# A second pair of accumulator banks for tile 5 of a two-MLP kernel, and six tiles ahead of the transpositions

## The chip, the cores and the metric

The kernel runs on one core of a Trainium2 chip. The metric is the time of one execution in device microseconds (us). The median of three runs stands for the kernel.

## The reference

Linear attention with decay feeds two MLPs in a row. Batch 4, 8 heads, 768 positions, head dimension 64, so 3072 tokens of width 512; the first MLP has 1024 hidden columns, the second 2048. All in float32.

```python
for t in range(S):
    state = gamma * state + einsum('bhd,bhe->bhde', k[:, :, t], v[:, :, t])
    y[:, :, t] = scale * einsum('bhd,bhde->bhe', q[:, :, t], state)
# x: (3072, 512)
h = x @ w_in                                   # first MLP, 512 -> 1024
sm = exp(h - max(h)) / (sum(exp(h - max(h))) + 1e-09)
solu = h * sm
x = ((solu - mean) / sqrt(var + 1e-06) * g_ln) @ w_out    # 1024 -> 512
h = x @ w_in2                                  # second MLP, 512 -> 2048
out = (h * cos(h)) @ w_out2                    # 2048 -> 512
```

## The kernel before

**Tiles.** The 3072 tokens are 24 tiles of 128 tokens (24 steps of the attention, each two batches by 64 positions), and six blocks of four tiles. Each float32 factor is split in a high and a low part, and each product is three matmuls (high by high, low by high, high by low).

**What one tile does.** `both(n)` does on TensorE the scores of step n+1 and the state of step n; VectorE then masks the scores (`masks`, two instructions, tile `in`) and ScalarE copies the state (`state_copy`, two instructions, tile `in`). `att_out(n)` makes the attention's output `y`, VectorE scales it to `x`, and ScalarE and VectorE split it into `xh` and `xl`. `first(n, c)` is the first layer of the first MLP for half c of its columns: four calls of `mm1`, each three matmuls of 128x512 (L543), so 24 matmuls for a tile, into two accumulator banks. `norm(n)` is then the row-wise normalisation: the maximum on VectorE (L561), the exponential on ScalarE, the product of both on VectorE (the last reader of the banks, an L332 row `u<-u,hA` or `u<-u,hB`, with a short row that reads its sum out), and further steps on the copy `u` in SBUF. Once four tiles of a block are normalised, `transp(g, j)` (L588) transposes column group j of the block, four transpositions of 128x128 each, into one of two banks `tr0` and `tr1`, which ScalarE and VectorE split into `lt` (L597, L599). `mm2(g, d)` (L612) is the second layer.

**Banks.** The banks of tile n are `hA` (two banks), or `hB` (two more) for tiles 1 and 3. `hB` lives in a pool of its own (`psb`, in the exit stack `boot`). `open_tr` closes this pool, and the two banks `tr0` and `tr1` are allocated in the place that it gives back. All these pools are opened with `reuse_waits="tile"`: the first writer of a new tile waits for all accesses to the old tile whose place it takes. The other banks are `y1` (one) and, for the attention, `sc`, `S` and `y` (three).

**The order.** The functions issue nothing; they enter operations into a plan with their engine, a cost, and the names that they read and write. `Plan.order` then writes out one order for all engines, by a list schedule over these costs and names. Each engine executes its part strictly in that order; the waits in the finished program come from the tiles that are really touched, not from the plan's names. TensorE's operations are taken from a window of the next ten in the order in which the code enters them, and the one with the smallest key goes first:

```python
for k, i in enumerate(pe[:self.WINDOW]):        # WINDOW = 10
    if need[i] == 0:
        t = max(free[e], ready_at[i])
        c.append((max(free[e], ready_at[i] + self.MARGIN) + k * self.STEP, t, i))  # 0.3, 0.05
```

So an operation that stands k places behind the first costs k times 0.05 us, and may overtake if it is ready earlier by more than that. VectorE and ScalarE take what can start first, and of that what has the longest path behind it; where nothing of the tiles is ready they take weight conversions (`convert`: rows `top`, `big`, `raw`, `o1h`, `o1l`, `w2a`).

**The order around the change.** Tiles 0 to 2 are entered by hand, then a loop enters tiles 3 to `EARLY` - 1, each as `first(n, 0)`, `first(n, 1)`, `attend()`; `attend` enters `both` and `att_out` of the tile two further on. Then the blocks follow. For block g, four more tiles (as far as there are any) are entered in eight halves (`part()`), between the transpositions and second layers of block g:

```python
transp(g, 0); transp(g, 1); part(); transp(g, 2); transp(g, 3); part()
mm2(g, 0, None, range(4)); transp(g, 4); transp(g, 5); part(); transp(g, 6); transp(g, 7); part()
mm2(g, 0, None, range(4, 8)); part(); part(); mm2(g, 1); part(); mm2(g, 2, ...); part(); mm2(g, 3)
```

With `EARLY` = 5, tile 5 is entered between the first transpositions, and the last block that has tiles to go with it (block 4) has three. `open_tr` is a step of the plan without cost, put in as soon as the operations that name `hB` have begun.

Of the kernel before, what the change touches and what calls it, by code (L numbers as in the profile page):

```python
# [34 lines left out]
K2 = FF2 // 128  # L35
NBLK = NT // 512
LAG = 3
EARLY = 5
UBUF = 7

INV2PI = 1.0 / (2.0 * math.pi)
# [197 lines left out]
def body(ctx: ExitStack, tc: tile.TileContext, qkv, consts,  # L239
# [40 lines left out]
    hA = ps1.tile([128, 2, 512], F32, name="hA")  # L280
# [3 lines left out]
    hB = psb.tile([128, 2, 512], F32, name="hB")  # L284
# [242 lines left out]
    p2 = {}  # L527

    def hbank(n, c):
        return (hB if n in (1, 3) else hA)[:, c], (("hB", c) if n in (1, 3) else ("hb", c))  # L530

    def h_of(n):
        return hB if n in (1, 3) else hA

    def mm1(n, c, k, ms=(0, 1, 2)):
        h, hk = hbank(n, c)
        xh, xl = xhs[n % 2], xls[n % 2]
        s = slice(c * 512, (c + 1) * 512)

        def mm():  # L540
            for m in ms:
                a, w = ((xh, w1h), (xl, w1h), (xh, w1l))[m]
                nc.tensor.matmul(out=h, lhsT=a[:, k], rhs=w[:, k, s], start=(k + m == 0), stop=(k == KD - 1 and m == 2))  # L543
        r = [("xh", n % 2)]
        if 0 in ms or 1 in ms:
            r += [("w1h", k, c)]
        if 1 in ms:
            r += [("xl", n % 2)]
        if 2 in ms:
            r += [("w1l", k, c)]  # L550
        P.add("PE", 0.2267 * len(ms), mm, r, [hk], lat=0.2267 * len(ms) + 0.25)

    def norm(n):
        b = [hbank(n, c) for c in (0, 1)]
        h = h_of(n)
        hk = [b[0][1], b[1][1]]
        sm = sms[n % 3]
        smk = lambda *c: [("sm", n % 3, x) for x in c]
        u = us[n % UBUF]
        uk = [("u", n % UBUF, c) for c in (0, 1)]  # L560
        P.add("DVE", 1.135, lambda: nc.vector.tensor_reduce(  # L561
            out=sm[:, 0:1], in_=h, axis=AX.XY, op=ALU.max, negate=True), hk, smk(0))
        act(u, h, AF.Exp, hk + smk(0), uk + smk(1), 1.1, 1.35, bias=sm[:, 0:1], accum_out=sm[:, 1:2])
        stt(u, u, 1.0, h, ALU.mult, ALU.mult, hk, uk + smk(2), 1.18, accum_out=sm[:, 2:3])
        ts(sm[:, 3:4], sm[:, 2:3], -1.0 / FF1, None, ALU.mult, None, smk(2), smk(3), 0.07)
        act(junk, u, AF.Square, uk + smk(3), [("junk",)] + smk(4), 1.14, 1.38, bias=sm[:, 3:4], accum_out=sm[:, 4:5])
        ts(sm[:, 5:6], sm[:, 1:2], 1e-9, None, ALU.add, None, smk(1), smk(5), 0.07)
        stt(sm[:, 6:7], sm[:, 5:6], 1e-6, sm[:, 5:6], ALU.mult, ALU.mult, smk(5), smk(6), 0.07, port=True)
        stt(sm[:, 7:8], sm[:, 4:5], 1.0 / FF1, sm[:, 6:7], ALU.mult, ALU.add, smk(4, 6), smk(7), 0.07, port=True)
        P.add("POOL", 0.56, lambda: nc.gpsimd.tensor_tensor(out=sm[:, 8:9], in0=sm[:, 7:8], in1=mhalf, op=ALU.pow),  # L570
              smk(7), smk(8), port=True)
        tt(sm[:, 9:10], sm[:, 3:4], sm[:, 8:9], ALU.mult, smk(3, 8), smk(9), port=True, occ=0.07)
        act(u, u, AF.Identity, smk(8, 9), uk, 1.14,
            alt=("DVE", 0.75, lambda: nc.vector.tensor_scalar(
                out=u, in0=u, scalar1=sm[:, 8:9], scalar2=sm[:, 9:10], op0=ALU.mult, op1=ALU.add), True),
            scale=sm[:, 8:9], bias=sm[:, 9:10])
# [214 lines left out]
    def attend():  # L791
        n = nxt[0]
        if n >= ns:
            return
        nxt[0] += 1
        if n == 0:
            load_to(0)
            prep(0)
            scores(0)
        load_to(n + 1)  # L800
        if n + 1 < ns:
            prep(n + 1)
            both(n)
        att_out(n)
        if n == ns - 1:
            p2["sb_hook"] = [P.add("HOOK", 0.0, open_sb, lat=0.0, after=P.using({"in", "amg", "sc", "S", "y"}))]

    def first(n, c):
        for k in range(KD):
            mm1(n, c, k)  # L810
        if c == 1:
            norm(n)
# [46 lines left out]
    attend()  # L859
    for n in range(3, EARLY):  # L860
        first(n, 0)
        first(n, 1)
        attend()
    nb = EARLY
    for g in range(NBLK - 1):
# [132 lines left out]
```

## Time and profile before

| | us |
|---|---|
| median of 3 runs | 900.62 |
| lowest and highest run | 896.74, 902.73 |
| the profiled execution, its own time | 899.53 |
| its span, first to last instruction | 897.7 |
| TensorE busy in it | 873.6 |

PE is TensorE's matmuls, DVE is VectorE, ACT is ScalarE, POOL is GpSimd, SP issues most DMAs. Times of rows are us from the start of the span unless marked ns. The profiled execution lies 1.1 us below the median.

### The profile page before, as it was taken

To read this page: it belongs to the slowest core of one execution; us is meant where nothing else is said; L and a number is where in the kernel's file an instruction comes from. 1 tells how busy PE (TensorE), PEld (TensorE's weight loads), DVE (VectorE), ACT (ScalarE), POOL (GpSimd) and SP (SyncE) were. 2 spreads that over 40 slices of the span, in tenths; PEclk is the share of its full clock that TensorE was granted. 3 is DMA by queue.
4 is the path that set the end of the run, shared out by engine and by line. 5 is a ranking of instruction groups with operands and counts; after the bars stand their busy time and mean duration, and the time that the engine had idled before them with its cause. 6 is when DMAs were issued, how large, how long until landed. Compare 5 with 4: busy or idle time off the path is not lost.

```text
span 897.7 us, 14593 instructions
## 1 busy us (share of the span) xinstructions
PE 873.6 (97%) x5888; PEld 722.6 (80%) x5888; DVE 571.2 (64%) x1014; ACT 421.5 (47%) x701; POOL 45.9 (5%) x62
## 2 busy tenths in 40 slices
PE   5998999999999999999999999999999999999997
PEld 4777888888888878888888888888888888888886
DVE  4989858587473665476656565656655565557553
ACT  4688746466452464353343343334433443334332
POOL 2111201011010000000000000000000000000000
PEclk9998999999999999999999999999999999999999
DMA  9993688888520141220020002001200120011002
GB/s 265 295 336 96 189 276 269 296 254 297 161 81 32 50 139 65 82 106 1 24 71 0 1 24 71 0 1 46 49 1 0 48 47 1 1 48 24 1 0 48
DMA packets 38660, 85.17 MB, mean 95 GB/s; under 512 B 5440, under 2 KB 5440, under 8 KB 38592
## 3 DMA queue, kind: packets, MB, share of 16 engines
q1 hardware_dynamic: 38224, 83.24, 29.9%
q10 hardware_dynamic: 368, 0.99, 0.4%
q8 instruction: 46, 0.75, 0.3%
q14 instruction: 22, 0.18, 0.1%
HBM read 64.29 MB, written 19.92 MB: 94 GB/s over the span
## 4 chain that ended last, share of the span: by engine, by line
PE 90%; DMA 4%; DVE 2%; ACT 2%; issue 0%; SPq 0%; ACTq 0%
PE h L681 29%; PE acc L718 29%; PE y L612 12%; PE hA L543 11%; DMA in<-qkv_dram 4%; PE tr L612 2%; PE tr L588 2%; PE y L455 2%; PE sc L390 1%; DMA big<-w_in_dram 1%; ACT junk L321 1%; ACT u L321 0%; DVE in L324 0%; DVE u L332 0%; DVE sm L561 0%; PE S L398 0%
## 5 line engine op out<-in xcount | busy, mean ns | idle before, releaser
L693 ACT ACTIVATE r<-r,hp 128x512 f32<-128x512 f32 x96 | 69.5, 724 | 158.8 <-DVE r L691 158.8
L695 DVE TENSOR_TENSOR r<-r,h 128x512 f32<-128x512 f32 x96 | 66.0, 687 | 65.2 <-ACT r L693 65.2
L612 PE MATMUL y<-lt,o1h 128*128 128x512 f32 x320 | 105.3, 397 | 0.7 <-ACT ys L617 0.7
L687 DVE SCALAR_TENSOR_TENSOR r<-ki,h 128x512 f32<-128x512 int32 x96 | 65.9, 686 | 56.4 <-ACT ki L685 56.4
L699 DVE TENSOR_TENSOR gl<-r,gh 128x512 fp32r<-128x512 f32 x96 | 66.3, 690 | 46.3 <-ACT gh L697 46.3
L718 PE MATMUL acc<-o2u,gh 128*128 128x512 f32 x288 | 94.5, 389 | 0.0
L718 PE MATMUL acc<-o2h,gh 128*128 128x512 f32 x240 | 93.4, 389 | 0.0
L718 PE MATMUL acc<-o2h,gl 128*128 128x512 f32 x240 | 93.4, 389 | 0.0
L718 PE MATMUL acc<-o2l,gh 128*128 128x512 f32 x240 | 93.4, 389 | 0.0
L685 ACT ACTIVATE ki<-h 128x512 int32<-128x512 f32 x96 | 57.4, 598 | 75.1 <-PE h L681 75.1
L697 ACT ACTIVATE gh<-r 128x512 fp32r<-128x512 f32 x96 | 60.5, 630 | 53.0 <-DVE r L695 53.0
L543 PE MATMUL hA<-w1h,xh 128*128 128x512 f32 x176 | 72.2, 410 | 8.9 <-DVE u L332 6.9
L681 PE MATMUL h<-yh,w1h 128*128 128x512 f32 x192 | 74.7, 389 | 0.0
L681 PE MATMUL h<-yh,w1l 128*128 128x512 f32 x192 | 74.7, 389 | 0.0
L681 PE MATMUL h<-yl,w1h 128*128 128x512 f32 x192 | 74.7, 389 | 0.0
L612 PEld LDWEIGHTS y<-lt,o1h 128*128 128x128 f32 x320 | 60.0, 188 | 14.6 <-ACT ys L617 1.2
L543 PE MATMUL hA<-w1h,xl 128*128 128x512 f32 x176 | 69.0, 392 | 0.0
L543 PE MATMUL hA<-w1l,xh 128*128 128x512 f32 x176 | 68.6, 394 | 0.0
L689 DVE SCALAR_TENSOR_TENSOR r<-ki,r 128x512 f32<-128x512 int32 x96 | 66.4, 691 | 3.1
L718 PEld LDWEIGHTS acc<-o2u,gh 128*128 128x128 f32 x288 | 54.0, 188 | 11.2
L612 PE MATMUL y<-lt,o1l 128*128 128x512 f32 x160 | 62.3, 390 | 0.0
L681 PE MATMUL h<-yh,w2a 128*128 128x512 f32 x192 | 59.5, 391 | 0.0
(108 smaller groups left out, 1687.6 us busy)
## 6 DMA issues: line engine op xcount, KB each, us to landing
in<-qkv_dram SPq DMA_DIRECT2D x48, 256.0 KB, 5.1
in<-qkv_dram SPq DMA_DIRECT2D x95, 128.0 KB, 4.7
raw<-w_in_dram SPq DMA_DIRECT2D x16, 511.8 KB, 6.1
raw<-w_out_dram SPq DMA_DIRECT2D x16, 511.8 KB, 4.7
y1d<-ys SPq DMA_DIRECT2D x24, 256.0 KB, 2.5
x<-y1d SPq DMA_DIRECT2D x24, 256.0 KB, 3.1
out_dram<-o SPq DMA_DIRECT2D x48, 128.0 KB, 2.4
kept_out<-wt SPq DMA_DIRECT2D x16, 256.0 KB, 3.6
```

The costliest lines, as they stand in the source:

```text
L455: nc.tensor.matmul(out=p_y[64 * par:64 * par + 64, j], lhsT=W[par][:, j], rhs=X[par][:, j], start=True, stop=True)
L543: nc.tensor.matmul(out=h, lhsT=a[:, k], rhs=w[:, k, s], start=(k + m == 0), stop=(k == KD - 1 and m == 2))
L612: nc.tensor.matmul(out=y1(), lhsT=w[:, j, ds], rhs=lts[j][:, a], start=(j + m == 0), stop=(j == K1 - 1 and m == 2))
L681: nc.tensor.matmul(out=p2["h2"][b], lhsT=w2tile(c, lo)[:, k, cs], rhs=p2[a][:, k], start=(k + m == 0), stop=(k == KD - 1 and m == 2))
L685: P.add("ACT", 0.5, lambda: nc.scalar.activation(out=p2["ki"][s], in_=p2["h2"][b], func=AF.Identity, scale=INV2PI, bias=0.25), [("h2", b)] ...
L687: P.add("DVE", 0.61, lambda: V.scalar_tensor_tensor(out=p2["r"][s], in0=p2["ki"][s], scalar=-C1, in1=p2["h2"][b], op0=ALU.mult, op1=ALU.ad ...
L689: P.add("DVE", 0.61, lambda: V.scalar_tensor_tensor(out=p2["r"][s], in0=p2["ki"][s], scalar=-C2, in1=p2["r"][s], op0=ALU.mult, op1=ALU.add ...
L693: P.add("ACT", 0.62, lambda: nc.scalar.activation(out=p2["r"][s], in_=p2["r"][s], func=AF.Sin, bias=hp[:, 0:1]), (), [("r", s)])
L695: P.add("DVE", 0.6, lambda: V.tensor_tensor(out=p2["r"][s], in0=p2["r"][s], in1=p2["h2"][b], op=ALU.mult), [("h2", b)], [("r", s)])
L697: P.add("ACT", 0.54, lambda: nc.scalar.activation(out=p2["gh"][g], in_=p2["r"][s], func=AF.Copy), [("r", s)], [("gh", g)])
L699: P.add("DVE", 0.6, lambda: V.tensor_tensor(out=p2["gl"][g], in0=p2["r"][s], in1=p2["gh"][g].bitcast(F32), op=ALU.subtract), [("r", s), (" ...
L718: nc.tensor.matmul(out=p2["acc"][t], lhsT=p2[a][g][:, ts_], rhs=o2tile(j, lo), start=(j == 0 and m == 0), stop=(j == K2 - 1 and m == 2))
```

## The change

Tile 5 gets the banks `hB` that tiles 1 and 3 have, and `EARLY` goes from 5 to 6, so that tiles 3, 4 and 5 are entered ahead of the first transposition. The name under which tile 5's banks are entered into the plan stays that of `hA` (`"hb"`), since the second part of `hbank` is not changed.

```diff
-EARLY = 5
+EARLY = 6
...
     def hbank(n, c):
-        return (hB if n in (1, 3) else hA)[:, c], (("hB", c) if n in (1, 3) else ("hb", c))
+        return (hB if n in (1, 3, 5) else hA)[:, c], (("hB", c) if n in (1, 3) else ("hb", c))
 
     def h_of(n):
-        return hB if n in (1, 3) else hA
+        return hB if n in (1, 3, 5) else hA
```

After it, the operations of TensorE are entered from tile 4 on as: tile 4's `both(6)` and `att_out(6)`, eight `mm1` of tile 5, `both(7)`, `att_out(7)`, `transp(0, 0)`, `transp(0, 1)`, half of tile 6, and so on; before, `transp(0, 0)` and `transp(0, 1)` stand ahead of tile 5's first half, `transp(0, 2)` and `transp(0, 3)` ahead of its second. Block 4 is left with two tiles to go with it.

## Rows read from the trace of the kernel before

**Rows 1.** The page: engines, busy us (share of the span) and instructions.
```profile
PE 873.6 (97%) x5888; PEld 722.6 (80%) x5888; DVE 571.2 (64%) x1014; ACT 421.5 (47%) x701; POOL 45.9 (5%) x62
```

**Rows 2.** Stretches of 10 us: length; busy us by engine (PE, PEld, DVE, ACT, POOL), clock, DMA.
```profile
60.00:70.00 10.00, 5.53 (x111) 4.48 (x109) 9.85 (x24) 9.45 (x16) 2.59 (x3) 0.91 1.04 330
70.00:80.00 10.00, 9.45 (x40) 7.80 (x40) 9.26 (x15) 8.28 (x16) 1.42 (x1) 0.75 0.08 23
...
110.00:120.00 10.00, 10.00 (x46) 8.29 (x45) 3.06 (x7) 3.67 (x8) 0.55 (x1) 1.00 0.67 229
```

**Rows 3.** Waits of PE, whole span: us in total, times, longest.
```profile
PE hA L543 <- DVE u L332: 6.9, 2, 5.0
...
PE y L612 <- ACT ys L617: 0.7, 1, 0.7
```

**Rows 4.** Timeline of PE: start, duration, operation, in brackets idle before it.
```profile
62.97 0.39 PE L543 MATMUL hA<-w1l,xh 128*128 128x512 f32 x1
...
64.38 1.15 PE L455 MATMUL y<-in 128*64 128x64 f32 x32
...
70.55 0.79 PE L543 MATMUL hA<-w1h,xh 128*128 128x512 f32 x1 [5.02 <-DVE u L332]
...
73.28 1.90 PE L588 MATMUL tr<-ident,u 128*128 128x128 f32 x8
...
77.09 1.03 PE L588 MATMUL tr<-ident,u 128*128 128x128 f32 x8
77.88 0.47 PE L543 MATMUL hA<-w1h,xh 128*128 128x512 f32 x1
...
79.81 0.40 PE L543 MATMUL hA<-w1l,xh 128*128 128x512 f32 x1
...
81.23 1.15 PE L455 MATMUL y<-in 128*64 128x64 f32 x32
82.31 0.50 PE L612 MATMUL y<-lt,o1h 128*128 128x512 f32 x1
```

**Rows 5.** Stretches of 1 us, columns as in the stretches of 10 us.
```profile
68.00:69.00 1.00, 0.00 (x0) 0.00 (x0) 0.99 (x2) 0.98 (x3) 0.15 (x1) 0.61 1.10 367
74.00:75.00 1.00, 1.00 (x7) 1.00 (x6) 0.42 (x2) 0.60 (x1) 0.00 (x0) 0.50 0.00 0
75.00:76.00 1.00, 1.00 (x6) 0.83 (x6) 0.84 (x2) 0.78 (x2) 0.00 (x0) 0.98 0.00 0
...
42.00:43.00 1.00, 1.00 (x5) 0.83 (x6) 0.97 (x2) 1.00 (x4) 0.00 (x0) 1.00 1.03 405
```

**Rows 6.** Timeline of DVE.
```profile
61.81 1.21 DVE L332 SCALAR_TENSOR_TENSOR u<-u,hB 128x1024 f32<-128x1024 f32 x1
...
67.67 1.38 DVE L324 TENSOR_TENSOR in<-sc,mg 64x512 f32<-64x512 f32 x2
...
69.27 1.22 DVE L332 SCALAR_TENSOR_TENSOR u<-u,hA 128x1024 f32<-128x1024 f32 x1
...
70.41 0.69 DVE L324 TENSOR_TENSOR x<-y,mg 128x512 f32<-128x512 f32 x1
...
75.00 0.69 DVE L599 TENSOR_TENSOR lt<-tr,lt 128x512 fp32r<-128x512 f32 x1 [0.58 <-ACT lt L597]
...
79.09 1.28 DVE L599 TENSOR_TENSOR lt<-tr,lt 128x512 fp32r<-128x512 f32 x2
80.29 1.21 DVE L561 TENSOR_REDUCE sm<-hA 128x1 f32<-128x1024 f32 x1
...
83.50 1.22 DVE L332 SCALAR_TENSOR_TENSOR u<-u,hA 128x1024 f32<-128x1024 f32 x1
```

**Rows 7.** Timeline of ACT.
```profile
68.83 1.20 ACT L321 ACTIVATE in<-S 64x512 f32<-64x512 f32 x2
...
81.81 1.07 ACT L321 ACTIVATE u<-hA,sm 128x1024 f32<-128x1024 f32 x1
```

**Rows 8.** Timeline of PE, the other wait for `hA` and the wait in block 4.
```profile
41.90 0.50 PE L543 MATMUL hA<-w1h,xh 128*128 128x512 f32 x1 [1.89 <-DVE u L332]
...
322.49 0.50 PE L612 MATMUL y<-lt,o1h 128*128 128x512 f32 x1 [0.74 <-ACT ys L617]
```

## The prediction, made before the changed kernel was run

> **What bounds the kernel now.** I read the page first: TensorE is busy for 97% of the span [rows 1], so an edit that adds and removes no matmul can win only idle time and time at a low clock. Next the stretches: nearly all of the idle time lies at the start, and the worst stretch near the change is 60 to 70 us, with PE busy for 5.53 of 10 us while DVE has 9.85 and ACT 9.45 [rows 2]. The following stretch has PE busy, but at a mean clock of 0.75. The waits name the place: PE waited for `hA` twice, 6.9 us in all, 5.0 us in one piece [rows 3]. In PE's timeline this is tile 5: `att_out(6)` ends at 65.53, and its first matmul starts at 70.55 [rows 4], when DVE's product of tile 4 (start 69.27, 1.22 us) has read `hA` [rows 6]. Tile 4's last matmul had ended at 63.36, so 7.1 us passed from it to the end of that product. DVE was not slow in a single row; it was full.
>
> The idle time has a second price. The clock was still full at first and fell to 0.50 (1.2 of 2.4 GHz) within 68 to 69, while PE stood still; it came back at 75 [rows 5]. PE worked from 70.55 to 75.0 at half speed: 4.45 us for 2.2 us' worth, a loss of 2.2 us. The other wait for `hA`, 1.89 us before 41.90 [rows 8], was followed by a clock of 1.00 [rows 5].
>
> So **5.0 + 2.2 = 7.2 us** is all there is at this place, 0.8% of the time. About 1% is what a measurement of this kernel can tell from no change (its three runs span 0.7%), so even the whole gain would hardly show.
>
> **A yardstick.** I count to one point: 82.31, where the second layer starts (L612) [rows 4]. From 65.53 to there PE did tile 5 (24 matmuls; nine of them go from 77.88 to 80.1, so 0.23 each and 5.5 us), `both(7)` (80.1 to 81.23, 1.2 with its start), `att_out(7)` (81.23 to 82.31, 1.1), and four calls of `transp` (two take 77.09 to 77.88, so 1.6 at full clock): 9.4 us of work. With 5.0 idle and 2.2 of clock that is 16.6 of the 16.8 us found. After 82.31 PE works without a wait until 321 [rows 3, 8], and DVE's queue runs empty by 110 to 120 (3.06 of 10 us) [rows 2], so what is won or lost at this point stays in the end time.
>
> **Part 1: tile 5 in hB.** These banks are free early: tile 3's product of `hB` ends at 63.0 [rows 6], before `att_out(6)` does. By the tiles, tile 5 could start at 65.53. But the order is the plan's, and the plan enters tile 5 still under the name of `hA`: it believes that tile 5 waits for tile 4's product. With `EARLY` 6 the window holds, behind the eight `mm1` of tile 5, `both(7)` as the ninth operation (before, it was the thirteenth, out of the window). `both(7)` waits for the masks of 67.67 [rows 6] and the state copies, which end at 70.03 [rows 7]; tile 4's product has read `hA` at 70.49. Eight places cost 8 x 0.05 = 0.4: keys 70.43 against 70.49. The plan's own times are shorter, but the order of these steps is that of the rows, and I take it that `both(7)` goes first, narrowly. Then PE, in order, stands before `both(7)` until 70.03, and tile 5's free banks don't help. `att_out(7)` needs `x` of 70.41 to 71.1 [rows 6] and stays behind tile 5.
>
> **Part 2: the transpositions behind tile 5.** `tr0` and `tr1` are allocated in the place of `hB`, and the first writer waits for every access to `hB`. Before, its last reader was tile 3's product (63.0), long done at 73.28. Now it is tile 5's. So `transp(0, 0)`, entered behind `att_out(7)`, waits until tile 5 is computed, its maximum and exponential are made, and its product has read the banks. The plan doesn't know of that wait (for it tile 5 is in `hA`), so it puts nothing in the gap; tile 6, whose real banks have been free since 70.5, stands behind the transposition on TensorE. **The wait is moved, not removed.** Behind it on TensorE is everything; ACT and DVE hold only `lt` and later steps there.
>
> Its size: both 1.2, tile 5 5.5, and the clock loss of 2.2 as before (the idle time of 4.5 us is nearly the old one): tile 5's last matmul ends at 70.03 + 8.9 = 78.95, `att_out(7)` at 80.05. From the last matmul to the end of the product it took tile 5 before 80.2 to 84.7, 4.5 us [rows 4, 6], and tile 4 7.1 us. The floor is 3.9: maximum from 80.29 (1.21), exponential from 81.81 (1.07 and its read-out) [rows 7], product 1.22 with its read-out. I take 4.5, since DVE's queue should be clear by then: from 70.41 to the maximum at 80.29 are 9.9 us, of which four `lt` rows (75.00 first, 79.09 last) took 2.7 and waits in front of them 0.7; the other 6.5 and the masks of `both(7)`, 1.4, end at 78.3. So the product ends at 83.45, PE is idle from 80.05 to there, 3.4 us, and four `transp` later it is 85.05 instead of 82.31: **+2.7 us**.
>
> The clock after this second stop: 1.89 us of idleness left it at 1.00 and 5.02 us halved it, and 3.4 lies between. Bounds 0 and 2.2; I take the middle, **+1.1**.
>
> If the plan puts tile 5 ahead of `both(7)`, the first wait does go: tile 5 runs from 65.53 to 71.0, `both` and `att_out` to 73.3. But its maximum keeps its place in DVE's queue behind the 6.5 us that the plan gives DVE for the time of tile 5, and DVE begins these at 70.49 in either case: maximum at 77.0, product read at 81.5, then 1.6 of transpositions and 2.2 of clock: 85.3, **+3.0**. So both orders come out alike: DVE's backlog sets the place.
>
> **Part 3: the rest.** Every tile after 5 uses `hA` as before, and the pattern between blocks repeats one tile later; the seven `u` buffers fit it, as tile 4g+7 is still entered behind block g's last transpositions. Block 4 has two tiles to go with it, not three; its cover already failed once, by 0.74 us, before the second layer's second column group [rows 8]. Bounds -0.7 (that wait gone) and +1.5 (one more such wait and a longer one); I take 0. `transp(0, 2)` may come right behind `transp(0, 1)` and wait for its bank to be emptied (the DVE row at 75.00 starts 1.7 us after its transposition and takes 0.69): 0 to +1.5, taken as 0, since half of tile 6 can stand between. Loads: step 8's are issued before 65 as before; nothing else moves past a queue.
>
> **Sum.** 899.5 (profiled execution) + 2.7 + 1.1 = 903.3; that execution lies 1.1 under the median, and from the median it is 904.4. I say **904**. The parts' bounds (-0.7 to +1.5 block 4, 0 to 1.5 `transp`, 0 to 2.2 clock, 3.9 to 7.1 product) give 901 to 910.
>
> **Rivals.** *The wait simply goes.* Tile 5 at 65.53, no idle time, full clock: 900.6 - 7.2 = 893.4. For it: `hB` is free at 63.0. Against: the place of `tr0`. The Trainium skill (Perfetto Trace Analysis, Matmuls) says that independent matmul groups should rotate through different banks, so that emptying one overlaps the next; by that rule this result follows, at 893.4. The trace agrees in so far as the one long wait is for a bank. Half of it would come if tile 5 went first and DVE took its maximum at once: product read at 71.0 + 4.5 = 75.5, the point at 77.1, 895.4. For that DVE would have to be free at 71, but it is filled from 60 to 80 [rows 2].
>
> *Both stops, and the second a long one.* The product of tile 5 takes as long behind the conversions as tile 4's did, 7.1 us: read at 86.05, then 1.6 and 2.2: 89.9, +7.6; with `transp(0, 2)` waiting as well, +9.1, **910**. It decides from the point where DVE's queue is longer than PE's 8.9 us of work. For it: DVE at 9.85 of 10 us; against: the sum of 78.3 above.
>
> *It does nothing*: the stops and the cover level out, within 1.5 us of 900.6. That needs the product read at 80.6.
>
> **Chances.** Moved wait, +1 to +6: 0.68. Nothing: 0.14. Wait gone, in whole or half: 0.10 (893 to 896). Long second stop: 0.08 (908 to 911). Leaving out the gain and the end of the long stop, the range is 898 to 909. Over 1% either way is below 891.6 and above 909.6: faster 0.02, slower 0.06, same 0.92.
>
> **What would show it.** Right: PE idle ahead of a `both` (L390) until about 70; tile 5 in `hB` after it; a new wait of PE at L588 for DVE's `u<-u,hB` at about 83; no wait on `hA` at 70. Wrong: L588 without a wait (the banks would not be shared as I read the code), or tile 5 starting at 65.5 and a product read before 80.

## The result, and the profile after

The changed kernel takes **905.93 us** (median of 10 runs, 903.76 to 909.42) against 900.54 for the kernel before in 10 runs: ratio **1.0064**, 95% interval 1.0047 to 1.0081. So it is slower by 5.4 us, inside the range of 898 to 909 and close to the 904 that was said. The profiled execution of the changed kernel has a span of 904.1 us. Of the ten runs the four at a mean granted clock of 0.990 took 907.06 to 909.42 us, the other six (0.991 to 0.995) 903.76 to 905.94, as did both profiled executions (905.94 and 904.78, at 0.993).

PE's waits in the changed kernel, whole span (columns as in [rows 3]):

```profile
PE sc L390 <- DMA in<-qkv_dram: 8.4, 2, 5.6
...
PE tr L588 <- DVE u L332: 4.2, 1, 4.2
PE hA L543 <- DVE u L332: 2.1, 2, 1.9
```

The 5.0 us wait of tile 5 for `hA` is gone. In its place stands a wait of 4.2 us at L588, the transposition, for DVE's product: a line that had no wait before. The wait of block 4 for `ys` [rows 3] is gone too.

PE's timeline around it, for comparison with [rows 4]:

```profile
66.55 1.15 PE L455 MATMUL y<-in 128*64 128x64 f32 x32
70.56 0.37 PE L390 MATMUL sc<-in 64*64 64x64 f32 x1 [2.86 <-DMA in<-qkv_dram]
...
71.70 0.37 PE L398 MATMUL S<-in 64*64 64x64 f32 x2 [0.66 <-ACT in L321]
...
73.60 0.79 PE L543 MATMUL hB<-w1h,xh 128*128 128x512 f32 x1
...
80.30 0.39 PE L543 MATMUL hB<-w1l,xh 128*128 128x512 f32 x1
80.61 1.15 PE L455 MATMUL y<-in 128*64 128x64 f32 x32
85.93 1.16 PE L588 MATMUL tr<-ident,u 128*128 128x128 f32 x8 [4.17 <-DVE u L332]
86.75 0.78 PE L543 MATMUL hA<-w1h,xh 128*128 128x512 f32 x1
...
97.09 0.50 PE L612 MATMUL y<-lt,o1h 128*128 128x512 f32 x1
```

Read it from the top. `att_out(6)` ends at 67.70. `both(7)` comes next, ahead of tile 5, as the plan's keys made likely: its scores wait until 70.56 for a load, its state until 71.70 for the state copies. Only then does tile 5 start, in `hB`, whose last reader had ended at 65.2. `att_out(7)` ends at 81.76, and the first transposition waits until 85.93. The last row is the start of the second layer, the point to which the prediction counts; here all of tile 6, `both(8)` and `att_out(8)` are done ahead of it.

DVE and ACT in the same stretch:

```profile
71.14 1.21 DVE L332 SCALAR_TENSOR_TENSOR u<-u,hA 128x1024 f32<-128x1024 f32 x1
...
80.72 1.23 DVE L561 TENSOR_REDUCE sm<-hB 128x1 f32<-128x1024 f32 x1 [1.91 <-PE hB L543]
81.86 0.68 DVE L324 TENSOR_TENSOR x<-y,mg 128x512 f32<-128x512 f32 x1
82.46 2.19 DVE L332 SCALAR_TENSOR_TENSOR o1l<-big,gcol,o1h 128x512 fp32r<-128x512 f32 x2
84.57 1.21 DVE L332 SCALAR_TENSOR_TENSOR u<-u,hB 128x1024 f32<-128x1024 f32 x1
```

```profile
81.98 1.11 ACT L321 ACTIVATE u<-hB,sm 128x1024 f32<-128x1024 f32 x1 [2.11 <-DVE sm L561]
82.99 0.20 ACT L321 ACTIVATION_READ_ACCUMULATOR u<-hB,sm 128x1 f32 x1
```

The maximum of tile 5 waited 1.91 us for PE, so DVE was clear by then, as the sum had it. The exponential is done at 83.19, but the product starts at 84.57: two weight conversions (`o1l`) stand between. It ends at 85.78, and PE starts 0.15 us later.

The granted clock, stretches of 1 us as in [rows 5]:

```profile
69.00:70.00 1.00, 0.00 (x0) 0.00 (x0) 0.99 (x5) 1.00 (x2) 0.55 (x1) 0.84 1.03 391
...
76.00:77.00 1.00, 1.00 (x5) 0.82 (x4) 1.00 (x2) 1.00 (x5) 0.00 (x0) 0.74 0.56 211
```
```profile
85.00:86.00 1.00, 0.07 (x1) 0.10 (x2) 0.79 (x2) 0.00 (x0) 0.00 (x0) 1.00 0.42 133
86.00:87.00 1.00, 1.00 (x9) 1.00 (x10) 0.00 (x0) 0.40 (x1) 0.00 (x0) 0.88 0.00 0
87.00:88.00 1.00, 1.00 (x4) 0.81 (x4) 0.77 (x2) 1.00 (x3) 0.00 (x0) 0.50 0.00 0
...
90.00:91.00 1.00, 1.00 (x6) 0.83 (x5) 0.59 (x6) 1.00 (x4) 0.00 (x0) 0.92 0.00 0
```

It fell twice, once for each stop. The second time it was full all through the stop, fell within 86 to 87, after PE had resumed, and came back within 90 to 91: some 3.2 us at half speed, 1.6 us lost.

### The profile page after: what moved, and what is told of

It reads as the page before. It is cut to its first block, busy times and chain, and to the rows that moved or that the text cites. A ratio compares the mean times of both kernels' runs of the same rounds, so it can differ in the third digit from the quotient of the medians.

```text
span 904.1 us, 14590 instructions
## 1 busy us (share of the span) xinstructions
PE 876.2 (97%) x5888; PEld 724.2 (80%) x5888; DVE 570.4 (63%) x1008; ACT 423.0 (47%) x707; POOL 45.9 (5%) x62
## 4 chain that ended last, share of the span: by engine, by line
PE 91%; DMA 5%; DVE 2%; ACT 1%; issue 0%; SPq 0%; ACTq 0%
PE h L681 29%; PE acc L718 29%; PE y L612 12%; PE hA L543 11%; DMA in<-qkv_dram 5%; PE tr L612 2%; PE tr L588 2%; PE y L455 2%; PE sc L390 1%; DMA big<-w_in_dram 1%; PE hB L543 1%; PE S L398 1%; DVE sm L561 0%; DVE u L332 0%; DVE o1l L332 0%; ACT in L321 0%
## 5 line engine op out<-in xcount | busy, mean ns | idle before, releaser
L695 DVE TENSOR_TENSOR r<-r,h 128x512 f32<-128x512 f32 x96 | 66.0, 687 | 65.2 <-ACT r L693 65.2
L543 PE MATMUL hA<-w1h,xh 128*128 128x512 f32 x168 | 69.1, 412 | 3.6 <-DVE u L332 2.1
L543 PE MATMUL hA<-w1h,xl 128*128 128x512 f32 x168 | 66.1, 394 | 0.0
L543 PE MATMUL hA<-w1l,xh 128*128 128x512 f32 x168 | 65.6, 395 | 0.0
```

Of the source, the lines that this page charges most:

```text
L695: P.add("DVE", 0.6, lambda: V.tensor_tensor(out=p2["r"][s], in0=p2["r"][s], in1=p2["h2"][b], op=ALU.mult), [("h2", b)], [("r", s)])
```

## The experiments

My theory: the wait was moved behind tile 5, onto the transpositions that take the place of `hB`; the plan's false name for tile 5's banks keeps the first stop as well; the queues of the other engines set when tile 5's product ends. Ratios are to runs of the kernel before on the same chip, with 95% intervals.

| Kernel | median us | before | ratio |
|---|---|---|---|
| changed | 905.93 | 900.54 | 1.0064 (1.0047 to 1.0081) |
| e1_early_only | 904.56 | 900.92 | 1.0047 (1.0026 to 1.0069) |
| e3_true_name | 898.89 | 900.92 | 0.9985 (0.9969 to 1.0002) |
| e4_tile5_first | 902.12 | 900.92 | 1.0018 (1.0000 to 1.0035) |
| e8_true_name_and_wait | 897.58 | 900.92 | 0.9963 (0.9946 to 0.9981) |
| e5_short_conversions | 903.39 | 901.43 | 1.0022 (1.0005 to 1.0040) |
| e6_tile5_first_short | 901.82 | 901.43 | 1.0008 (0.9994 to 1.0021) |
| e11_keep_busy | 904.28 | 901.43 | 1.0024 (1.0011 to 1.0037) |
| e9_seven_ahead | 913.57 | 901.43 | 1.0141 (1.0121 to 1.0162) |
| e13_before_busy | 900.17 | 901.37 | 0.9986 (0.9973 to 0.9999) |

**One half of the change alone.** The kernel before with

```diff
-EARLY = 5
+EARLY = 6
```

> Tile 5 stays in hA, EARLY is 6: the order of all engines is that of the changed kernel, only tile 5's banks differ. My theory (the wait for tile 5's product stands in PE's order in both, and DVE's queue sets when it ends): the first two transpositions start at once after att_out(7), at about 82, and tile 6's first matmul waits in their place, until about 86; PE wins the 0.8 us of two transp calls at most, so 904.5 to 906, like the changed kernel. Rival A (the shared place of hB and tr0 is what costs): the loss goes with it, about 901.

1.0047: the loss stays without `hB`. PE's timeline shows the wait one step further on, at tile 6's first matmul for the banks of tile 5:

```profile
82.21 1.09 PE L588 MATMUL tr<-ident,u 128*128 128x128 f32 x8
...
86.36 0.50 PE L543 MATMUL hA<-w1h,xh 128*128 128x512 f32 x1 [3.06 <-DVE u L332]
```

Two transpositions go ahead of it, and the rest is as in the changed kernel. So rival A falls: the shared place decides which instruction waits, not that one waits. With overlapping intervals (1.0047 and 1.0064), a cost of the banks themselves isn't shown; the loss comes with the new order. The other half alone (`hB` for tile 5, `EARLY` 5) wasn't tried: transpositions would stand ahead of tile 5's first use of the banks whose place they take.

**The true name.** The change, and

```diff
-        return ..., (("hB", c) if n in (1, 3) else ("hb", c))
+        return ..., (("hB", c) if n in (1, 3, 5) else ("hb", c))
```

> The change, and tile 5 is entered into the plan under the name of hB too. My theory (the plan's false name makes it put both(7) ahead of tile 5 and DVE's work ahead of tile 5's maximum): tile 5 starts at about 67.6 with no idle time in front and no fall of the clock, its product is read near 80, nine matmuls of tile 6 stand ahead of the first transposition, whose wait falls from 4.2 to about 2 us; 897 to 900, faster than both kernels. Rival B (one more tile ahead of the transpositions costs by itself, whatever the banks): 904 or more.

898.89, at the edge of what was said, and 0.8% below the changed kernel in ratio. Tile 5 now follows `att_out(6)` at once, and the first transposition waits 4.65 us, not 2 (the `sm` row that it waits for is the short one on DVE right behind the product of `hB` and its read-out):

```profile
62.94 1.15 PE L455 MATMUL y<-in 128*64 128x64 f32 x32
64.02 0.50 PE L543 MATMUL hB<-w1h,xh 128*128 128x512 f32 x1
...
78.89 1.51 PE L588 MATMUL tr<-ident,u 128*128 128x128 f32 x6 [4.65 <-DVE sm L328]
```

One stop is left of two, and the clock falls for it as before (0.50 from 78 to 84). Rival B falls: with the same six tiles ahead, the kernel is not slower than before.

**The true name and the wait.** In addition, `transp` is entered as a writer of `hB`:

```diff
-... [("hb", 2 + s)], lat=0.65, after=p2["tr"])
+... [("hb", 2 + s), ("hB", s)], lat=0.65, after=p2["tr"])
```

> As with the true name, and the plan is also told that the first two transpositions wait for the last reader of hB: 15 matmuls of tile 6 instead of nine stand ahead of the first transposition. My theory: the wait at the first transposition is under 1 us, 0 to 2 us better than with the true name alone, 895.5 to 899. Rival B: 904 or more.

897.58, ratio 0.9963: 0.4% faster than the kernel before, 1.0% faster than the changed one. The plan now puts 15 matmuls of tile 6 ahead of the transposition, and the clock is never below 1.00 from 60 to 120:

```profile
66.21 0.50 PE L543 MATMUL hB<-w1h,xh 128*128 128x512 f32 x1
...
80.30 1.06 PE L588 MATMUL tr<-ident,u 128*128 128x128 f32 x8 [2.51 <-DVE sm L328]
```
```profile
70.00:80.00 10.00, 7.79 (x120) 6.08 (x118) 9.92 (x16) 9.62 (x18) 2.38 (x2) 1.00 0.67 198
```

The wait that is left is 2.51 us, not under 1. DVE and ACT are full (9.92 and 9.62 of 10 us).

**Tile 5 first.** The change, with `both(7)` and `att_out(7)` entered so that they may start only after tile 5's `mm1`:

```diff
-              r1 + r2, w1 + w2, lat=1.55)
+              r1 + r2, w1 + w2, lat=1.55, after=tile5(n))
```

(the same for `att_out`; `tile5(7)` is the list of tile 5's operations).

> The change, and the plan is told to put both(7) and att_out(7) behind tile 5. My theory (DVE's queue sets the place of tile 5's product): tile 5 starts at about 67.6, PE is done with it and att_out(7) at about 75.4, the first transposition waits until about 83, a wait of 7 to 8 us; 2 to 3 us less than the changed kernel, 902.5 to 904.5, still slower than before. Rival C (DVE is free and takes the maximum at once): product read at about 78, 897 to 899.

902.12, as expected of the theory: better than the change, not better than before. PE starts tile 5 at 66.38, right behind `att_out(6)`, and stands once, for longer:

```profile
73.79 0.52 PE L460 MATMUL y<-in 128*64 128x64 f32 x12
81.73 1.94 PE L595 MATMUL tr<-ident,u 128*128 128x128 f32 x8 [7.42 <-DVE u L332]
```

Line numbers are seven higher here. DVE begins the maximum at 77.21, five microseconds after tile 5's last matmul. Rival C falls.

**Shorter conversions.** All rows `o1l` shortened from 512 to 8 columns (the others are set to zero once, at the start), in the changed kernel and in the one with tile 5 first:

```diff
-            stt(lo, full, s, hi.bitcast(F32), ...)
+            stt(lo[:, 0:8], full[:, 0:8], s, hi[:, 0:8].bitcast(F32), ...)
```

> The changed kernel with the same order, but the rows that make the low part of the second layer's weights (o1l on VectorE, 0.7 us each) work on 8 of 512 columns; the rest of that low part is zero, so the output lacks its share. My theory (what stands in DVE's queue sets when tile 5's product ends): tile 5's maximum still waits for PE, but the two o1l rows (2.2 us) between maximum and product are gone, so the product starts when the exponential ends, 1.4 us earlier, and the kernel takes 1 to 2 us less, 904 to 905. Rival D (DVE's queue is not what holds the product): no change, 905.5 to 906.5.

903.39: in ratio 0.42% below the changed kernel, some 3.8 us, more than expected. The wait fell from 4.17 to 2.83 us, the 1.35 us that was due, and the clock did not fall after this shorter stop (1.00 in 80 to 90), which I had not counted. The wait and the 1.6 us of clock together are 3.0 us; the rest isn't explained (the rows are shorter in the whole kernel, not only here). Rival D falls here:

```profile
84.87 1.06 PE L588 MATMUL tr<-ident,u 128*128 128x128 f32 x8 [2.83 <-DVE u L332]
```
```profile
80.00:90.00 10.00, 7.17 (x68) 5.98 (x67) 6.81 (x16) 5.67 (x11) 1.04 (x1) 1.00 0.20 52
```

> Tile 5 ahead of both(7), and the low part of the second layer's weights made on 8 of 512 columns only (the output lacks the rest). Here DVE, not PE, holds tile 5's maximum. My theory: four o1l rows ahead of the maximum are gone, 2.7 us, of which ACT's queue may give back a part; the wait at the first transposition falls from 7.4 to 5 us, and the time by 2 to 3 us, 899 to 900.5. Rival D: no change, 902.

901.82: 0.1% below the kernel that it is to be compared with (1.0008 against 1.0018), where 2 to 3 us were expected, and the intervals overlap: they allow the 2 us and no change at all. The wait fell from 7.42 to 5.30 us, close to the 5 that was said, but more than half of that doesn't come from the shorter rows: `att_out(6)` ends 3.5 us ahead of the end of tile 4's product in this profile, 4.65 us in e4's, so PE comes later to its wait. Here my theory was too simple. Tile 5's product ends 9.6 us after tile 4's, 10.5 with the whole rows. DVE, relieved of 2.0 us of work between tile 4's product and tile 5's maximum, waits for ACT, which makes the high parts:

```profile
81.73 1.94 PE L595 MATMUL tr<-ident,u 128*128 128x128 f32 x8 [5.30 <-DVE u L332]
```
```profile
76.12 0.23 DVE L332 SCALAR_TENSOR_TENSOR o1l<-big,gcol,o1h 128x8 fp32r<-128x8 f32 x1 [0.47 <-ACT o1h L321]
76.76 0.23 DVE L332 SCALAR_TENSOR_TENSOR o1l<-big,gcol,o1h 128x8 fp32r<-128x8 f32 x1 [0.41 <-ACT o1h L321]
76.90 1.22 DVE L568 TENSOR_REDUCE sm<-hB 128x1 f32<-128x1024 f32 x1
```

So the order on both engines sets the place of the maximum, not DVE's rows alone.

**The price of the clock.** PE kept busy in the second stop of the changed kernel by matmuls into a bank that nobody reads yet:

```diff
+            for _ in range(16 if n in (7,) else 0):
+                nc.tensor.matmul(out=y1s, lhsT=w1h[:, 0, 0:128], rhs=w1h[:, 0, 0:512], start=True, stop=True)
```

> The changed kernel, with 16 matmuls more of 128x512 (3.6 us) into the idle bank of the second layer, right behind att_out(7); nobody reads them. They fill most of the second stop, so the wait for tile 5's product ends at the same time, but PE is not idle ahead of it. My theory (the second stop also costs a fall of the clock): granted clock stays 1.00 after it, and the time falls by 1.5 to 2.2 us, 903.7 to 904.5. Rival E (the fall of the clock costs nothing here): 905.9 or more.

904.28; in ratio 0.4% less than the changed kernel, with a rest of the wait of 0.32 us and the clock at 1.00 after it:

```profile
70.13 0.37 PE L398 MATMUL S<-in 64*64 64x64 f32 x2 [0.84 <-ACT in L321]
...
83.56 1.06 PE L590 MATMUL tr<-ident,u 128*128 128x128 f32 x8 [0.32 <-DVE u L332]
```
```profile
80.00:90.00 10.00, 9.68 (x52) 7.93 (x51) 8.21 (x17) 6.58 (x13) 1.42 (x1) 1.00 0.18 54
```

Useless work in a stop made the kernel faster, so the fall had a price, and rival E falls. Its size isn't shown by the medians. The two ratios are 3.6 us apart, and their intervals (1.0047 to 1.0081 and 1.0011 to 1.0037) don't meet; the rows show 1.6. In this profile the first stop is shorter too, 67.8 to 70.13 instead of 67.70 to 71.70, and the slow stretch behind it ends at 73.2 instead of 76.5; the 16 matmuls stand behind both, so this is not their doing.

The same in the kernel before, 18 matmuls behind `att_out(6)`:

> The kernel before, with 18 matmuls more of 128x512 (4.1 us) behind att_out(6), into the idle bank of the second layer; nobody reads them. They fill most of the old 5.0 us stop; tile 5 still starts when tile 4's product is read. My theory (the stop costs 2.2 us more through the clock): the granted clock stays 1.00 from 65 to 80, and the time falls by 1.5 to 2.5 us, ratio 0.997 to 0.9985. Rival E (the fall costs nothing): ratio 1.000.

0.9986 (0.9973 to 0.9999): 1.2 us, between 0.1 and 2.4. The clock was 1.00 from 60 to 120, and 0.81 us of the stop was left. The 2.2 us of the prediction lie at the edge.

**Seven tiles ahead.** As with the true name and the wait, and `EARLY` 7.

> True name and known wait, and EARLY is 7: all of tile 6 and att_out(8) stand ahead of the first transposition. My theory: tile 5's product is read before PE gets to the first transposition, so that wait is gone, but tile 6's matmuls were the cover there already and tile 7 now waits for hA behind DVE's queue; 895.5 to 899, within 1.5 us of the kernel with six. Rival B (each tile more ahead of the transpositions costs by itself): 900 or more.

913.57, and the time says nothing about rival B. The last four transpositions of block 0 read `u0` after tile 7 has taken it over (tile 7 is then entered ahead of them, and there are seven buffers), so part of the computation is done on other data, and these transpositions wait for tile 7's normalisation (5.8 us at L588 for `u` of L574). I had overlooked that; my statement that the seven buffers fit holds for six tiles ahead only.

**Chance in the first 60 us.** A second profile of each kernel:

> The kernel before once more, for a second profile: where att_out(6) ends. It was 65.5 in the first profile and 67.7 in that of the changed kernel, whose order on TensorE is the same up to there. If that is chance (DMA landings in the first 20 us), this profile may lie anywhere from 64 to 68; if the changed order on VectorE costs it, near 65.5.

> The changed kernel once more, for a second profile. att_out(6) ends near 67.7 if the changed order on VectorE costs it; anywhere from 64 to 68 if it is chance. The wait ahead of the first transposition stays at 3.5 to 4.5 us in either case.

`att_out(6)` ends at 65.5 and 67.3 in the two profiles of before, at 67.7 and 64.95 in the two of after. So its place is chance, and the part behind it can be compared: to the end of the span it is 832.2 and 834.2 us before, 836.4 and 838.1 after, **4.0 us** more in the mean. The stop of before was 5.0 and 6.0 us; the second stop of after was 4.17 in both.

## Why the prediction was right, point by point

- *What bounds it.* Right: what the change cost and gave back are waits of PE and time at a low clock, and no experiment that kept both MLPs whole won more than 0.4%. The 1% below which nothing was to be told was too wide: with ten runs of each kernel the 0.6% is clear.
- *Tile 5 in hB, behind both(7).* Right, and shown: the rows have that order, and entering the true name (e3) removes the first stop. That it was narrow (70.43 against 70.49) was worked out from rows, not from the plan's own times, and no run shows it. What I didn't see is that `both(7)` also waits for a load (step 8's, 2.86 us of the stop in the profile). The state copies ended later, so its price is nothing here.
- *The moved wait.* Right: L588 waits for `u<-u,hB`. e1 corrects the reason in one point: without the shared place, the next user of `hA` waits in its stead, and the loss is much the same. What counts is that the plan had nothing else to give PE until tile 5's product was read.
- *Its size, +2.7.* Right in sum, by two misses that level out, which is luck. PE's waits are 2.86 + 0.66 + 4.17 = 7.7 us against 5.0 before, 2.7 more. But the first stop was 4.0 us (67.70 to 71.70), not 4.5, and the second 4.17, not 3.4: the product ended 5.1 us after tile 5's last matmul, not 4.5, because two conversions stood between exponential and product; e5 shows these 1.4 us.
- *The clock, +1.1.* Mis-sized: it was the middle between nothing and 2.2, and the rows show 1.6 behind the second stop. Behind the first it is 2.4 (71.70 to 76.5 at half speed), where 2.2 as before was said.
- *The sum.* From the end of `att_out(6)` to the second layer (67.70 to 97.09) are 29.4 us, of which tile 6, `both(8)` and `att_out(8)` take 7.7 at the rates of [rows 4]. That leaves 21.7, against 16.8 before: +4.9, where 2.7 + 1.1 was said. The wait of block 4 is gone (-0.7, the end that I gave as the lower bound; in e1 and in the second profile of the change it is gone as well). So +4.2, which is the difference of the first two profiles (836.4 to 832.2); the mean of the two pairs is 4.0. The medians differ by 5.4 (4.2 to 7.3). What they have beyond the profiles stays open: none of the four runs at a clock of 0.990 has a profile.
- *Tile 5 first, +3.0.* Too high: 1.6 us (0.0 to 3.2) in e4. And its reason, that DVE's backlog alone sets the place, doesn't stand in that form (e6).
- *The rival that the wait simply goes.* It is what the Trainium skill's rule (Perfetto Trace Analysis, Matmuls), to rotate independent groups through different banks, would have given. The runs show what it hangs on here: with the order unaware of the second pair, the pair won nothing (1.0064 with it, 1.0047 without, in the same order); with an order made for it (e8), the kernel won 0.4%, of the 0.8% at that place.

## What to carry to other kernels

Where an order is planned from names and executed with waits taken from the real buffers, a buffer changed without its name is planned as if nothing had changed, and any wait that it brings is invisible to the plan. When a buffer is shared in time, ask who gets its place next and what the engine could do meanwhile; and count a stop of TensorE with the slow stretch behind it, where the rows show one (the 5.02 and 4.17 us had one, the 2.83 us of e5 had none).

## What was unexpected

The clock fell after the second stop, not in it: full from 80 to 86 in the changed kernel, where PE stood still from 81.8 to 85.9, and 0.50 from 87 to 90, while PE worked without a gap. In the first stop (67.7 to 70.6) it had fallen within 69 to 70, while PE stood still. So the clock of the stop's own slices doesn't tell whether it will be paid for.
